# Attention before a routed expert layer: keys and queries turned on VectorE, 32x32 score tiles, one early expert phase

## The chip, the core and the metric

The kernel runs on one core of a Trainium2 chip. It uses TensorE (PE: matmuls and transposes), VectorE (DVE), ScalarE (ACT), GpSimd (POOL), SyncE (SP) and 16 DMA engines. The metric is the time on the device from the start to the end of one execution, in microseconds (us); lower is better. Profile and times come from different executions.

## What is computed

Eight batches of eight heads with 576 tokens of 64 dimensions, 32 rows p for each head. First p attends to k and v, which gives 32 packed rows a head; then every q attends to the packed rows. The result, 4608 rows of 512, goes through a layer of eight experts, of which each row takes the best one.

```python
def sm_attn(qq, kk, vv):
    s = scale * np.matmul(qq, kk.transpose(0, 1, 3, 2))
    s = s - np.max(s, axis=-1, keepdims=True)
    a = np.exp(s)
    a = a / (np.sum(a, axis=-1, keepdims=True) + 1e-09)
    return np.matmul(a, vv)
p_packed = sm_attn(p, k, v)
out = sm_attn(q, p_packed, p_packed)
...
logits = x @ w_gate + modality_bias[modality_id]
e_idx = np.argmax(logits, axis=1)
...
    h = np.maximum(x[mask] @ w1[e], 0.0)
    out[mask] = gate_w[mask, None] * (h @ w2[e])
```

Everything is fp32. With the data of the runs the rows go to three of the eight experts.

## The kernel before

**Attention.** The eight batches are four pairs, the heads two groups of four: eight units of work (pair i, group g), each 2 batches x 4 heads x 576 tokens. `load_tok` brings k and q of a unit as 128 partitions x 4 tokens (512 tokens of a batch, L199, runs of 1024 B) and the 64 left-over tokens of both batches apart (L195, runs of 256 B); `load_v` does the same for v (L220, L222). `relayout` copies each batch's tokens so that heads come behind tokens, k on ACT (L207), q on DVE (L209). `trans` turns them on PE, three 128x128 transposes at a time (L229), and ACT copies the turned block out of PSUM (L233). `scores1` multiplies p's rows with the turned keys (L242, tiles of 64 columns), takes the maximum (L247), the negated maximum (L250) and the exponential with its sum (ACT, L254). `a1trans` turns the weights on PE (L266), ACT copies them (L269), `pack` multiplies them with v (L279, tiles of 32 columns) and divides by the sum (L284, into `bd`, where every head stands in its own half). `packT` turns the packed rows (L293), `gate` gives the heads' share of the logits (L304). `scores2` multiplies packed rows and turned queries (L315). DVE turns the scores by 32x32 blocks (L321), takes the maximum over the 32 packed rows (L324), subtracts (L326), ACT takes the exponential (L328), DVE sums (L331), adds 1e-9 and inverts (L333, L335), multiplies (L337) and turns back (L340). `xpart` multiplies with `bd` (L354): 128 columns of x and 8 of logits. ACT copies x out (L362), DVE the logits (L366), SP writes x to the scratch tensor `x_scr` in DRAM (L374, L379).

**Routing.** For each pair `routing` adds up the logits (L423), takes the best expert, ranks the rows of an expert by a scan and a matmul, and scatters each row's number and weight into the expert's list `lst` by nine indirect DMAs on POOL (L467).

**Experts.** Work is cut into *slots*: two tiles of 128 rows of one expert; with this data there are 20, three of them of one tile only. `table_phase` works out on DVE which slot is whose. `fetch` reads the slot's list (`mt`, L657) and gathers its rows of x (L659, two indirect DMAs) on POOL. `st_x` turns the rows on PE (L672) and splits them in a high and a low part (ACT L674, DVE L675); `st_1` does x @ w1 as three products of parts (L685), with relu and split (L689, L690); `st_2` does the second product (L719), the weight (L723) and the indirect write of the rows (L724). For three one-tile slots there is another form (L703). Expert weights come by SP (2 MB each) and are split by ACT (L652) and DVE or POOL (L653) into `w1h`, `w1l`, `w2h`, `w2l`.

**Order.** PE, DVE, ACT and SP take their instructions in program order. For the attention the order is the string `ORDER` (L404 to L408), walked once a unit; a `>` before a step's name means the unit one later. The experts run in three phases (`NA`, `SA`): phase a has two slots and needs the rows of the first two pairs only, phase b goes on to slot 6 with the rows of three pairs, phase c takes the rest. So slots 0 and 1 stand in PE's program ahead of the last attention units, whose steps follow between their matmuls (`run_all`).

## Time and profile before

| | |
|---|---|
| three runs | 643.27, 644.70 and 644.98 us, median 644.7 |
| the profiled execution, first to last instruction | 658.5 us |
| PE busy in it | 598.8 us |
| DVE, ACT, POOL busy | 261.5, 238.6, 156.2 us |
| DMA bytes | 87.11 MB |
| mean granted TensorE clock | 0.961 |

The profiled execution is longer than the runs without a profile; sums against the trace are made in its own time. Busy time is that of any instruction on the engine. A row of a timeline reads: start, length, engine, line, operation, output <- input, shape, count, and in brackets the idle time before it and what ended that. A row of groups reads: line, engine, operation, output <- input, forms, count, then busy time, mean ns of one, and the idle time just before them with its releasers. PE's tile sizes stand as rows*columns.

### The profile page before, as it was taken

The numbers are of one execution on the slowest core, as the hardware profiler recorded it, in microseconds if no ns is written. First come the engines' busy times: TensorE is split into PE (matmuls) and PEld (weight loads), VectorE is DVE, ScalarE is ACT, GpSimd is POOL, SyncE is SP. The second block draws the span as 40 slices with busy tenths as digits, with TensorE's granted clock in tenths as the row PEclk, the third lists the DMA queues.
The fourth block names the chain that finished last, engine by engine and source line by source line (L and its number), as shares of the span: only waits on it lengthen the run. The fifth ranks groups of instructions, "written<-read, shape, count | busy, mean of one in ns | idle before, by whom it ended". The sixth has DMA issues, their size and how long they took to land. (4 is left out here: it accounts for less than half of the span.)

```text
span 658.5 us, 12203 instructions
## 1 busy us (share of the span) xinstructions
PE 598.8 (91%) x4564; PEld 505.9 (77%) x4564; DVE 261.5 (40%) x670; ACT 238.6 (36%) x457; POOL 156.2 (24%) x204
## 2 busy tenths in 40 slices
PE   3899969868689989999999999999999999999983
PEld 3565646535478968889888988998899899889982
DVE  1488958769955422112612016311120121112181
ACT  4677847756612202121612127221121221222271
POOL 3001050256161171211221322221122112122121
PEclk9999988968779998999999999999999999999998
DMA  9989999934843811111590212720110111112011
GB/s 239 277 200 274 314 303 300 292 92 146 317 148 105 295 30 63 49 49 33 198 397 30 66 50 66 290 66 34 50 49 34 50 50 53 45 50 51 35 50 53
DMA packets 74856, 87.11 MB, mean 132 GB/s; under 512 B 26448, under 2 KB 60240, under 8 KB 74768
## 3 DMA queue, kind: packets, MB, share of 16 engines
q1 hardware_dynamic: 64656, 63.79, 32.6%
q0 software_dynamic: 8528, 21.93, 10.6%
q8 instruction: 47, 0.77, 0.5%
q10 hardware_dynamic: 1584, 0.28, 0.2%
q14 instruction: 41, 0.34, 0.2%
HBM read 66.74 MB, written 19.24 MB: 131 GB/s over the span
## 5 line engine op out<-in xcount | busy, mean ns | idle before, releaser
L685 PE MATMUL ps_h<-x_hl,w1h 128*128 128x256 f32 x1088 | 202.1, 287 | 5.7 <-issue 4.9
L685 PEld LDWEIGHTS ps_h<-x_hl,w1h 128*128 128x128 f32 x1088 | 174.4, 195 | 8.5 <-issue 5.9
L685 PE MATMUL ps_h<-x_hl,w1l 128*128 128x256 f32 x544 | 155.8, 286 | 0.9 <-issue 0.8
L690 DVE SCALAR_TENSOR_TENSOR hl<-ps_h,hh 128x512 fp32r<-128x512 f32 x68 | 46.9, 690 | 263.8 <-ACT hh L689 261.4
L719 PE MATMUL ps_o<-w2h,hh 128*128 128x512 f32 x296 | 118.0, 399 | 2.8 <-ACT ot L723 1.6
L719 PE MATMUL ps_o<-w2h,hl 128*128 128x512 f32 x296 | 116.8, 395 | 0.0
L719 PE MATMUL ps_o<-w2l,hh 128*128 128x512 f32 x296 | 115.8, 391 | 0.3 <-DVEq L844 0.3
L685 PEld LDWEIGHTS ps_h<-x_hl,w1l 128*128 128x128 f32 x544 | 106.1, 195 | 1.5 <-issue 1.4
L689 ACT ACTIVATE hh<-ps_h 128x512 fp32r<-128x512 f32 x68 | 40.6, 597 | 179.0 <-PE ps_h L685 148.0
L724 POOL DMA_INDIRECT out_dram<-ot,mt x37 | 40.5, 1096 | 189.0 <-ACT ot L723 120.7
L723 ACT ACTIVATE ot<-ps_o,mt 128x512 f32<-128x512 f32 x37 | 25.4, 687 | 141.3 <-PE ps_o L719 115.1
L659 POOL DMA_INDIRECT xt<-x_scr,mt x46 | 45.0, 979 | 104.0 <-PE ps_t L672 45.2
L719 PEld LDWEIGHTS ps_o<-w2h,hh 128*128 128x128 f32 x296 | 55.7, 188 | 14.2 <-ACT ot L723 2.5
L719 PEld LDWEIGHTS ps_o<-w2h,hl 128*128 128x128 f32 x296 | 55.6, 188 | 11.6
L719 PEld LDWEIGHTS ps_o<-w2l,hh 128*128 128x128 f32 x296 | 55.7, 188 | 10.9 <-DVEq L844 0.6
L233 ACT COPY kT<-ps 128x384 f32<-128x384 f32 x96 | 44.0, 489 | 37.7 <-PE ps L229 20.4
L467 POOL DMA_INDIRECT lst<-meta,dsi x36 | 35.3, 980 | 83.2 <-DVE starts L522 31.4
L675 DVE TENSOR_TENSOR x_hl<-ps_t,x_hl 128x512 fp32r<-128x512 f32 x42 | 27.5, 683 | 19.7 <-ACTq L844 14.8
L229 PE MATMUL ps<-ident,rek 128*128 128x128 f32 x144 | 25.7, 306 | 10.3 <-POOL meta L114 7.0
L354 PE MATMUL ps<-bd,a2T 64*128 64x136 f32 (+1 forms) x320 | 28.7, 313 | 5.0 <-DVE lt L366 4.7
L657 POOL DMA_DIRECT2D mt<-lst x23 | 17.3, 752 | 61.9 <-DMA out_dram<-ot,mt 48.2
L229 PEld LDWEIGHTS ps<-ident,rek 128*128 128x128 f32 x144 | 17.9, 154 | 17.0 <-POOL meta L114 7.0
(189 smaller groups left out, 706.4 us busy)
## 6 DMA issues: line engine op xcount, KB each, us to landing
raw<-in_moe_w_dram SPq DMA_DIRECT2D x24, 1024.0 KB
raw<-in_k_dram SPq DMA_DIRECT2D x16, 512.0 KB
raw<-in_q_dram SPq DMA_DIRECT2D x16, 512.0 KB
ld_v<-in_v_dram SPq DMA_DIRECT2D x16, 512.0 KB
x_scr<-xs SPq DMA_DIRECT2D x16, 512.0 KB
rek<-in_k_dram SPq DMA_DIRECT2D x16, 64.0 KB
req<-in_q_dram SPq DMA_DIRECT2D x16, 64.0 KB
ld_v<-in_v_dram SPq DMA_DIRECT2D x16, 64.0 KB
```

Source lines behind the costliest of these rows:

```text
L229: nc.tensor.transpose(out=t[:, c * P:c * P + P], in_=D_[nm + "r"][:, c0 + c, 2 * pr:2 * pr + 2, :], identity=ident)
L233: nc.scalar.copy(out=T_[:, pr, c0 * P:c0 * P + 3 * P], in_=t[:, :3 * P])
L354: nc.tensor.matmul(xp[rows, pr, z * XW:z * XW + XW], a2T[rs, t0:t0 + n], D_["bd", u][rs, :], start=True, stop=True)
L467: ins = ins_of(nc.gpsimd.indirect_dma_start(out=lst, out_offset=bass.IndirectOffsetOnAxis(ap=dsi[:, c:c + 1], axis=0), in_=meta[:, i * NC ...
L659: ins.append(nc.gpsimd.indirect_dma_start(out=xt[:, t], out_offset=None, in_=x_scr[0:NA[ph] * 2 * S] if ph < 2 else x_scr, in_offset=bass. ...
L675: iv = tt(out=M["xl"][:, :, ts], in0=ps, in1=M["xh"][:, :, ts].bitcast(F32), op=ALU.subtract)
L685: nc.tensor.matmul(ps[:, f], M[a][:, j, (f0 + f) * P:(f0 + f) * P + P], M[b][:, j], start=(n == 0), stop=(n == 3 * KD - 1))
L689: ia = nc.scalar.activation(out=M["hh"][:, fs], in_=ps, func=AF.Relu)
L690: iv = nc.vector.scalar_tensor_tensor(out=M["hl"][:, fs], in0=ps, scalar=0.0, in1=M["hh"][:, fs].bitcast(F32), op0=ALU.max, op1=ALU.subtract)
L719: nc.tensor.matmul(op, M[a][:, j, t * P:t * P + P], M[b][:, j, :], start=(n == 0), stop=(n == 3 * KF - 1))
L723: nc.scalar.activation(out=ot, in_=op, func=AF.Copy, scale=mt.bitcast(F32)[:, t, 2:3])
L724: nc.gpsimd.indirect_dma_start(out=out, out_offset=bass.IndirectOffsetOnAxis(ap=mt[:, t, 1:2], axis=0), in_=ot, in_offset=None, bounds_che ...
```

## The change

**Loads.** All three tensors come as 64 partitions x 9 tokens for each batch, two batches one above the other (new `load`, L212, runs of 2304 B, two DMAs a tensor). The left-over tokens and the copies of `relayout` are gone. x is kept in two scratch tensors, one for each group of heads, and written by one DMA a unit (new L366, 9360 B a partition).

**Turning.** Instead of PE's transposes and ACT's copies, DVE turns k and q by 32x32 blocks (new `turn`, L220, 128x1152, four for each unit). A head dimension of 64 then lies in two blocks of 32 partitions.

**Scores.** New `scores` (L230) makes both score products from 32x32 tiles: 32 matmuls of 288 columns, 16 positions, two accumulated (64 instructions in the trace, as fp32 matmuls are counted twice). The packed product (L285) and the x product (L354) use 64x64 tiles.

**Second softmax.** The scores come out with tokens in the free dimension in the order that the x product wants. The maximum is a reduce with transposition (L331, four a unit, 128x9 from 128x288), spread by a transpose of a broadcast input (L335); one subtraction (L339) and one exponential (L344) follow. x is stored undivided, with two sums of weights for each pair of heads, got as two more columns of `bd` (`XW` = 130). `routing` divides the logits (L393 to L402) and `st_x` the rows of x (L659 to L662: add, reciprocal, multiply) before it turns them.

**Gathers.** `fetch` has four gathers a slot (L645, a tile from each of the two scratch tensors) where there were two.

**Phases.** One early phase b (three pairs, six slots) replaces a and b. All of attention and the routing of all four pairs stand ahead of the first expert matmul in PE's program.

The core of the diff:

```diff
-    NA = (NP // 2, NP - 1)
-    SA = [max(0, -((E * (P2 - 1) - m * 2 * S) // P2)) for m in NA]
+    NA = NP - 1
+    SA = -((E * (P2 - 1) - NA * 2 * S) // P2)
...
+        def load(src, nm):
...
+            for u in range(2):
+                nc.sync.dma_start(t[64 * u:64 * u + 64].rearrange("p h c d -> p h (c d)"),
+                                  src[2 * i + u, hs].rearrange("h (p c) d -> p h (c d)", c=NC))
...
+        def turn(nm, z):
...
+            nc.vector.transpose(out=D_[nm + "T"][:, 2 * z:2 * z + 2].rearrange("p h c b q -> p (h c b q)"),
+                                in_=D_[nm][:, 2 * z:2 * z + 2].rearrange("p h c d -> p (h c d)"))
...
+        def scores(l, r, nm):
+            t = [ps.tile([P, 2, 512], F32, name="ps") for u in range(2)]
+            for db in range(2):
+                for h in range(HG):
+                    for u, hf in QD:
+                        qd = slice(32 * (2 * u + hf), 32 * (2 * u + hf) + 32)
+                        nc.tensor.matmul(t[u][32 * h:32 * h + 32, hf, :HS].rearrange("p (c q) -> p c q", c=NC),
+                                         l[qd, db, 32 * h:32 * h + 32], r[qd, h, :, db, :],
+                                         start=(db == 0), stop=(db == 1), skip_group_check=True)
...
+            for hf in range(2):
+                nc.vector.tensor_reduce(m2[:, hf], s2[:, hf, :HS].rearrange("p (c q) -> p c q", c=NC),
+                                        axis=AX.X, op=ALU.max, apply_transpose=True)
...
+            nc.vector.transpose(out=mB.rearrange("p f c q -> p (f c) q"),
+                                in_=m2.rearrange("p f c -> p (f c)")[:, :, None].broadcast_to([P, 2 * NC, 32]))
...
+            nc.vector.tensor_tensor(out=a2.rearrange("p c f q -> p f c q"),
+                                    in0=s2[:, :, :HS].rearrange("p f (c q) -> p f c q", c=NC), in1=mB,
+                                    op=ALU.subtract)
...
-        for t in range(2):
-            ins.append(nc.gpsimd.indirect_dma_start(
-                out=xt[:, t], out_offset=None, in_=x_scr[0:NA[ph] * 2 * S] if ph < 2 else x_scr,
+        for t in (1, 0):
+            for g in range(2):
+                ins.append(nc.gpsimd.indirect_dma_start(
+                    out=xt[:, t, g], out_offset=None, in_=x_scr[g] if ph else x_scr[g][0:NA * 2 * S],
...
+            nc.vector.tensor_scalar_add(rs[:, :, :, 0], xr[:, :, P:XW], 1e-9)
+            nc.vector.reciprocal(rs, rs)
+            xn = M["xn", t]
+            tt(out=xn.rearrange("p (a h d) -> p a h d", a=4, h=2), in0=xr[:, :, 0:P].rearrange("p a (h d) -> p a h d", h=2),
+               in1=rs.broadcast_to([P, 4, 2, D]), op=ALU.mult)
...
+            if i == NA - 1:
                 E0.append(val(E0[1], 0, 0, (ET.SP,), 0, E - 1))
                 load_w(W, 0, E0[2])
...
+                T.append((yield from table_phase("b", E0[0], NA, None, SA)))
...
+                for n in range(2):
+                    pre(n)
+                    yield
+                for z in range(4):
+                    split_w(W, 0, nc.gpsimd, (z,))
+                    yield
```

**DVE in a unit.** Before, from the second scores of one unit to its last turned block (`st` is the score block, `m` its maximum, `dn` the sum, `mx` and `nb` belong to the next unit's first softmax):

```order
L321 STREAM_TRANSPOSE st<-ps_1009 128x288 x2
L326 TENSOR_TENSOR st<-st,m_1023 128x576
L247 TENSOR_REDUCE mx<-ps_1036 128x1
L250 TENSOR_SCALAR nb<-mx 128x1
L331 TENSOR_REDUCE dn<-st 128x18
L247 TENSOR_REDUCE mx<-ps_1045 128x1
L333 TENSOR_SCALAR dn<-dn 128x18
L250 TENSOR_SCALAR nb<-mx 128x1
L324 TENSOR_REDUCE m_1079<-st 128x18
L335 RECIPROCAL dn<-dn 128x18
L326 TENSOR_TENSOR st<-st,m_1079 128x576
L337 TENSOR_TENSOR st<-st,dn 128x576
```

Now, from the spread packed rows (`pc`, what packT turns) to the unit's last subtraction (`a2T`, L339); the two L242 are the next unit's:

```order
L183 TENSOR_TENSOR pc<-bd_119 128x2x64 x2
L242 TENSOR_REDUCE nb<-ps 128x1
L220 STREAM_TRANSPOSE qT<-raw 128x1152
L242 TENSOR_REDUCE nb<-ps 128x1
L220 STREAM_TRANSPOSE kT<-raw 128x1152
L331 TENSOR_REDUCE m_609<-ps 128x9 x2
L331 TENSOR_REDUCE m_612<-ps 128x9 x2
L335 STREAM_TRANSPOSE mB<-m_609 128x576
L335 STREAM_TRANSPOSE mB<-m_612 128x576
L253 TENSOR_SCALAR r_556<-r_556 128x2
L254 RECIPROCAL r_556<-r_556 128x2
L339 TENSOR_TENSOR a2T<-ps,mB 128x2x9x32 x2
```

The exchange of sums and divisions for turns of k and q is seen here; the maximum of the next unit's first softmax stands between the turns.

**PE in a unit.** Before, from one unit's x products to the next one's first scores:

```order
L354 MATMUL ps_694<-bd,a2T 128x136 x4
L229 MATMUL ps_699<-ident,rek 128x128 x3
L229 MATMUL ps_703<-ident,rek 128x128 x3
L315 MATMUL ps_718<-kT,ppT 64x288 x4
L229 MATMUL ps_723<-ident,rek 128x128 x3
L229 MATMUL ps_733<-ident,rek 128x128 x3
L315 MATMUL ps_739<-kT,ppT 64x288 x4
L229 MATMUL ps_744<-ident,req 128x128 x3
L229 MATMUL ps_756<-ident,rek 128x128 x3
L242 MATMUL ps_761<-kT,pT 64x288 x4
```

Now a whole unit:

```order
L268 MATMUL ps<-ident,a_787 128x128 x8
L354 MATMUL ps<-bd_119,a2T 64x146 x24
L274 MATMUL ps<-ident,a_787 128x128
L354 MATMUL ps<-bd_119,a2T 64x146 x12
L285 MATMUL ps<-ld_v,a1T 64x128 x36
L230 MATMUL ps<-kT,pT 32x288 x32
L301 MATMUL ps<-ident,pc 128x128 x2
L314 MATMUL ps<-wg_124,ppT 32x16 x16
L230 MATMUL ps<-qT,ppT 32x288 x32
```

The transposes of k and q between the scores are gone; the first scores of a unit stand right behind the packed product of the one before.

**POOL before the first slots.** Before, the scatters of two pairs, the low parts of the first weights, and the lists and gathers of slots 0 and 1 (nine scatters of the third pair come behind them):

```order
L467 DMA lst<-meta,dsi 38912x4 x18
L653 TENSOR_TENSOR w1l<-raw_114,w1h 128x4x256 x4
L628 TENSOR_LOAD tab_a
L657 ISA
L657 DMA mt_2321<-lst 128x2x4
...
L659 DMA xt_2325<-x_scr,mt_2321 128x512 x2
L659 DMA xt_2326<-x_scr,mt_2322 128x512 x2
```

Now:

```order
L449 DMA lst<-meta,dsi 38912x4 x27
L638 TENSOR_TENSOR w1l<-raw_115,w1h 128x4x256 x2
L613 TENSOR_LOAD tab_b
L642 ISA
L642 DMA mt_100<-lst 128x2x4
...
L645 DMA xt_104<-x_scr_63,mt_100 128x260
L645 DMA xt_104<-x_scr_64,mt_100 128x260
...
L645 DMA xt_105<-x_scr_63,mt_101 128x260
L645 DMA xt_105<-x_scr_64,mt_101 128x260
L449 DMA lst<-meta,dsi 38912x4 x3
```

Ahead of the first list there are now the scatters of three pairs, and eight gathers in place of four ahead of the first expert matmul; in DVE's program the routing of pairs 1 to 3 and both tables stand behind the last unit's L339 (pair 1's from its second half on).

More of the change, by code (lines that the diff above doesn't have):

```diff
@@ L59, in packed_attn_moe_kernel @@
     sm = ctx.enter_context(tc.tile_pool(name="sm", bufs=4))
-    x_scr = dram.tile([N, DM], F32, name="x_scr")
+    XW = P + 2
+    XL = XW + 2 * E
+    GW = 2 * XW
+    x_scr = [dram.tile([N, GW], F32, name=f"x_scr{g}") for g in range(2)]
     lst = dram.tile([E * R, 4], I32, name="lst")
@@ L170, in prep_p @@
-    def prep_p(ps1, n4):
-        t = ps1.tile([P, 512], F32, name="ps1")
+    bds = [cw.tile([P, 2, XL], F32, name=f"bd{n}") for n in range(2)]
+    for t in bds:
+        for u in range(2):
+            nc.gpsimd.tensor_copy(out=t[:, u, P:XW], in_=mask[:, :, 0])
+    wg4 = cw.tile([P, 2, HG, 2, 2, E], F32, name="wg4")
+    nc.gpsimd.memset(wg4, 0.0)
+    wgt = cw.tile([P, 4 * HG, E], F32, name="wgt")
+    nc.gpsimd.memset(wgt, 0.0)
+    for u in range(2):
+        nc.scalar.dma_start(wgt[64 * u:64 * u + 32], w_gate.rearrange("(n p) e -> p n e", p=32))
@@ new lines, in packed_attn_moe_kernel, with more, step @@
+        todo = [rest()]
+        def more():
+            while todo:
+                try:
+                    next(todo[0])
+                    return
+                except StopIteration:
+                    todo.pop(0)
+        def step(m, nm):
+            next(us[m][nm])
+            if m == 0 and nm == "dk":
+                load_p(nc.scalar, 0, 2)
+                load_p(nc.scalar, 2, NP)
+            if m == 1 and nm == "dk":
+                for _ in prep_p(A["ps"], 2, nc.gpsimd):
+                    pass
+            if m == 0 and nm == "k0":
+                for _ in prep_p(A["ps"], 0, nc.vector):
+                    pass
+            if nm == "w0" and m % 2 and m // 2 < NA:
+                todo.append(route(m // 2))
```

562 lines of the change are left out of this document (243 added, 319 removed), and 4 rows, old and new, of the table ORDER.

## The prediction

> **What bounds the kernel now.** The page first: engines, then the slices.
>
> ```profile
> span 658.5 us, 12203 instructions
> PE 598.8 (91%) x4564; PEld 505.9 (77%) x4564; DVE 261.5 (40%) x670; ACT 238.6 (36%) x457; POOL 156.2 (24%) x204
> PE   3899969868689989999999999999999999999983
> DMA  9989999934843811111590212720110111112011
> ```
>
> PE is busy almost throughout, but for two reasons. The DMA row is full for some ten slices (attention) and nearly empty later (experts). The windows by stage separate them: one attention unit (from one pack's end to the next), the first expert slots after the attention, and eight later slots.
>
> ```profile
> 59.87:78.47 18.60, 17.13 (x213) 11.08 (x211) 15.70 (x43) 13.66 (x32) 0.00 (x0) 1.00 1.10 315
> 240.00:262.00 22.00, 18.00 (x116) 17.11 (x115) 2.21 (x4) 3.14 (x6) 8.12 (x9) 0.84 0.16 49
> 431.36:617.40 186.04, 186.04 (x1211) 169.68 (x1210) 31.68 (x48) 37.86 (x64) 37.80 (x40) 1.00 0.15 47
> ```
>
> After the length the columns are PE, PEld, DVE, ACT, POOL, granted clock, DMA share, GB/s. The eight slots leave PE no gap: 186.04/8 = **23.3 us a slot**, and the change leaves these matmuls alone (the same 20 slots in the same order). In the attention the DMA engines are over 100% busy with PE close behind. So the change can act on when the experts start and on their first slots, not on their rate.
>
> ```profile
> 181.02 1.01 PE L685 MATMUL ps_h<-x_hl,w1h 128*128 128x256 f32 x3
> 240.57 0.40 PE L685 MATMUL ps_h<-x_hl,w1h 128*128 128x256 f32 x2
> 244.07 0.40 PE L685 MATMUL ps_h<-x_hl,w1h 128*128 128x256 f32 x2 [1.13 <-issue]
> 246.18 0.60 PE L685 MATMUL ps_h<-x_hl,w1h 128*128 128x256 f32 x2 [1.59 <-issue]
> ```
>
> The first expert matmul is at 181.0. Slots 0 and 1 last until slot 2 starts at 240.57: 59.6 us where two slots alone take 46.5, because the last attention units run between their matmuls. From 240.57 to the span's end are **417.9 us**. At its head slot 2 stalls and runs at a lower clock (0.84 in the window), 6 to 7 us in all.
>
> **The new attention unit.** The old ones end their packs (L284) here:
>
> ```profile
> 22.78 0.61 DVE L284 SCALAR_TENSOR_TENSOR bd<-ps,r,mask 128x128 f32<-128x128 f32 x2 [2.02 <-PE ps L279]
> 42.32 0.59 DVE L284 SCALAR_TENSOR_TENSOR bd<-ps,r,mask 128x128 f32<-128x128 f32 x2
> 59.87 0.57 DVE L284 SCALAR_TENSOR_TENSOR bd<-ps,r,mask 128x128 f32<-128x128 f32 x2
> 78.47 0.58 DVE L284 SCALAR_TENSOR_TENSOR bd<-ps,r,mask 128x128 f32<-128x128 f32 x2
> 102.08 0.57 DVE L284 SCALAR_TENSOR_TENSOR bd<-ps,r,mask 128x128 f32<-128x128 f32 x2
> ```
>
> So 17.5 to 19.5 us a unit, and 23.6 where a pair's routing falls in. Transfers first:
>
> ```profile
> q1 hardware_dynamic: 32326, 25.74, 102.1%
> q1 hardware_dynamic: 1286, 3.28, 87.2%
> ```
>
> The first row is the attention from 50 to 140 us (packets, MB, share): 25.74/(90 x 1.021) = 280 GB/s in runs of 1024 and 256 B, 16.8 us for a unit's 4.72 MB. The second is an expert's weights, 335 to 345 us, in 4096 B packets: 376 GB/s. The new loads have runs of 2304 B, the x writes 9360 B; between the two rows I take 354 GB/s, **13.4 us** for 4.74 MB. [...]
>
> The work that goes, and the rows for what comes:
>
> ```profile
> L229 PE MATMUL ps<-ident,rek 128*128 128x128 f32 x144 | 25.7, 306 | 10.3 <-POOL meta L114 7.0 <-DMA rek<-in_k_dram 2.2 <-ACT rek L207 0.5
> L229 PE MATMUL ps<-ident,req 128*128 128x128 f32 x144 | 25.5, 299 | 1.7 <-issue 1.6
> L233 ACT COPY kT<-ps 128x384 f32<-128x384 f32 x96 | 44.0, 489 | 37.7 <-PE ps L229 20.4 <-remote 6.7 <-issue 6.1
> L207 ACT COPY rek<-raw 128x1024 f32<-128x1024 f32 x16 | 16.4, 1086 | 3.8 <-DMA raw<-in_k_dram 3.8
> L321 DVE STREAM_TRANSPOSE st<-ps 128x288 f32<-128x288 f32 x32 | 13.5, 459 | 13.7 <-remote 11.8 <-PE ps L315 1.8
> L340 DVE STREAM_TRANSPOSE a2T<-st 128x576 f32<-128x576 f32 x16 | 12.4, 777 | 0.4 <-DVEq L826 0.3
> L247 DVE TENSOR_REDUCE mx<-ps 128x1 f32<-128x576 f32 x16 | 12.1, 755 | 15.7 <-remote 8.9 <-PE ps L304 3.3 <-PE ps L242 3.0
> L326 DVE TENSOR_TENSOR st<-st,m 128x576 f32<-128x576 f32 x16 | 12.0, 750 | 0.1
> L324 DVE TENSOR_REDUCE m<-st 128x18 f32<-128x576 f32 x16 | 11.9, 741 | 0.0
> L284 DVE SCALAR_TENSOR_TENSOR bd<-ps,r,mask 128x128 f32<-128x128 f32 x16 | 4.7, 330 | 2.0 <-PE ps L279 2.0
> 45.67 1.19 PE L315 MATMUL ps<-kT,ppT 128*64 128x288 f32 x8
> 55.77 1.62 PE L279 MATMUL ps<-ld_v,a1T 128*32 128x64 f32 x80
> ```
>
> Gone are 51 us of PE's transposes (L229) and 60 of ACT's copies (L233, L207): over eight units 6.4 and 7.6 us each. ACT is then far from bounding. DVE becomes the chain of a unit. From the end of a pack to the last subtraction (new L339) it does, in its order: two products and two spreads (0.33 each by L284: 1.3), maximum (0.76), one turn of q, maximum (0.76), one turn of k, four reduces with transposition, two broadcast transposes (0.78 each by L340: 1.6), the reciprocal (0.3) and two subtractions (0.75 by L326: 1.5). A turn of 1152 columns isn't in the trace: 288 columns take 459 ns and 576 take 777, so 1.10 ns a column, 1.41 us each, 2.8 for two (bounds: 1.2 and 2.8 for both, from one column a ns and from two passes). Nor is a reduce that transposes: half of L324 is 0.37, that and a transpose (L321) 0.83; I take 0.41, 1.6 for the four, since the transpose alone costs no more than a pass. Sum **10.6 us**.
>
> The next pack waits for that subtraction: both want a PSUM buffer, and of the four the ninth allocation of a unit falls on what L339 reads. Then PE does the last transpose of the weights, a third of the x products and the pack of 72 instructions. L279 needs 1.62/80 = 20 ns an instruction with four tiles at once; by that spacing, stretched to 128 columns, 72 x 0.028 = 2.0, and 1.4 for the rest: 3.4. The other two turns (2.8) lie under these 3.4. So **T = 14.0 us a unit**, DVE busy for 13.4 of it, transfers 13.4.
>
> The scores now are 64 instructions in 32x32 tiles. L279 shows four column tiles at once, L315 two columns of 64 (0.149 us each, 0.30 for one tile's stream). Sixteen at once: 64 x 0.30/16 = 1.2 us; four: 4.8. I take 1.3 (64 x 20 ns), hidden behind the spreads, as the row shows column tiles running apart. [...]
>
> **Until the last unit.** The first pack's end stays at 22.8: the same first loads, two turns in place of copies and transposes. Seven units to 120.8, 10.6 to the subtraction, and 4 of routing that lie on DVE (the period with routing was 5 longer): sub(7) at **135.4**.
>
> **The tail.** Nothing of the experts is on PE before now. Its pieces are POOL's:
>
> ```profile
> 125.24 0.96 POOL L467 DMA_INDIRECT lst<-meta,dsi  x1 [31.39 <-DVE starts L522]
> 126.50 0.96 POOL L467 DMA_INDIRECT lst<-meta,dsi  x1 [0.30 <-issue]
> 136.78 4.66 POOL L653 TENSOR_TENSOR w1l<-raw,w1h 128x1024 fp32r<-128x1024 f32 x2
> 154.91 1.56 POOL L657 DMA_DIRECT2D mt<-lst  x2
> 158.92 1.03 POOL L659 DMA_INDIRECT xt<-x_scr,mt  x1 [2.44 <-DMA mt<-lst]
> 163.15 0.94 POOL L659 DMA_INDIRECT xt<-x_scr,mt  x1 [0.30 <-issue]
> L423 DVE TENSOR_REDUCE lg<-lt 128x72 f32<-128x288 f32 x4 | 2.6, 652 | 0.1
> L430 DVE TENSOR_TENSOR eq<-eq,desc 128x72 f32<-128x72 f32 x4 | 0.9, 234 | 0.1
> L675 DVE TENSOR_TENSOR x_hl<-ps_t,x_hl 128x512 fp32r<-128x512 f32 x42 | 27.5, 683 | 19.7 <-ACTq L844 14.8
> ```
>
> The rest of routing(1), some 20 dependent instructions (0.65, then 0.23 to 0.45) and a step on PE: 6.6. Eighteen scatters at 1.26: 22.8. Two w1l 4.7, two mt 1.6, again 4.7 and 1.6; table b on DVE (some 90 instructions of 0.2) is done by then. Four gathers of slot 0, 5.2, and four of slot 1, 5.2: DVE divides slot 1's rows before the second half of slot 0, so both count. Landing 2.4 (the wait in the 158.92 row), two divisions and the second low part 2.5 (0.68 each and two small ones). Sum **57.3**: first full expert matmul at 192.7, 11.7 after before's. On the way PE idles.
>
> Nothing then lies between slots 0 and 1: 46.5 in place of 59.6. Slot 2's stall partly goes; a cold clock at the experts' start and the doubled gathers come. Of the 6 to 7 us I give back 2.5 (bounds 0 and 5). Span: 192.7 + 46.5 + 417.9 - 2.5 = **654.6 us**, against 658.5. The runs had a median of 644.7, 0.979 of the profiled span: **641 us**, 0.6% less. The end is the same: the last slot, with its output, is in the 417.9.
>
> **Rivals.**
> - *Slower: the reduces with transposition (L331).* At the upper bound of 0.83 they add 1.7 us to the chain, eight times: 13.5 us, 668, **654**. They decide from 0.2 us each on, as everything after waits. For it: both operations are full passes in the rows; against: the transpose L321 is itself a pass of the same length as a reduce.
> - *Slower: 32x32 tiles in fours.* The scores take 4.8; DVE waits 3.5 after the spreads and 1.5 before the reduces, 5 us a unit, 35 in all: **675**. It counts from 1.3 us on. For it: no row has small tiles in both directions; against: each direction alone overlaps.
> - *The change doesn't do what it says:* the loads stay at 280 GB/s, a unit at 16.8 to 17: 21 us more, 676, **661**. [...] Against it stand the weights' 376 GB/s.
> - *Faster:* PE and DVE follow at the starts' spacing, T = 13.3 (5 us less), and slot 2's whole stall goes (4): 645.6, **632**. For it: in the rows of one engine starts lie some 0.07 closer than the durations; against: before's units were 0.7 to 2.7 over their largest need of 16.8.
>
> **How the numbers follow.** Forecast 0.40 (637 to 646), faster rival 0.20, reduces 0.20, loads 0.10, tiles 0.07, others 0.03. A measurement of this kernel can tell 0.3% from no change, 2 us. Faster takes 0.28 of the forecast and the faster rival: 0.48. Same takes 0.10 and a part of the rivals' near ends: 0.15. Slower the rest: 0.37. The range runs from 629 (a little beyond the faster rival) to 661, and leaves the tiles out above and the rest below.
>
> **What would show it.** A pack every 14.0 us with DVE over 90% busy and q1 above 340 GB/s; scores in 1.3 us; reduces (L331) at 0.41; 18 scatters in one row after the last subtraction, then w1l, mt and eight gathers; the first expert matmul near 193, slot 2 about 46 to 48 us later, and from there the same 23.3 a slot. Wrong it is if the units run over 15.5 us, or if scatters of pair 1 already run under the last units (the tail then shrinks by up to 11), or if slot 2 still stalls.

## The result and the profile after

| | before | after |
|---|---|---|
| median of the runs, us | 643.99 (4 runs) | 739.99 (4 runs, 732.47 to 746.33) |
| profiled execution, span, us | 658.5 | 744.6 |

The change makes the kernel slower: ratio 1.145, 95% interval 1.138 to 1.152. The ratio leaves out the slowest of after's runs, 746.33 us, and that one is the profiled execution. A few us of its 744.6 are therefore its own: two kernels below with the same attention have their last subtraction at 175.6 and 175.8 us, after has it at 179.6. What is said below of causes rests on the experiments too. The forecast was 641 us, with a range from 629 to 661.

The forecast was 654.6 us of span, so 90 us are to be found. First the page of after: busy time, then the slices for PE, the granted clock and the DMA engines.

```profile
span 744.6 us, 13666 instructions
PE 573.0 (77%) x5428; PEld 491.0 (66%) x5428; DVE 295.0 (40%) x649; ACT 188.4 (25%) x339; POOL 201.5 (27%) x234
PE   2676566686101999999987599799999999999871
PEclk9879876988555799999998799799999999999997
DMA  9999969952636401111390111451111111112111
```

PE had 91% before and has 77% now. It is half idle in the first ten slices, where the DMA row is full, and idle for two slices behind them (the tail). Small holes stand in the experts. Each of the three is placed by a few rows of the timeline: the subtractions of the attention units (DVE, start and length), then POOL and PE.

```profile
40.37 1.40 DVE L339 TENSOR_TENSOR a2T<-ps,mB 128x576 f32<-128x576 f32 x2
58.00 1.40 DVE L339 TENSOR_TENSOR a2T<-ps,mB 128x576 f32<-128x576 f32 x2
...
179.63 1.42 DVE L339 TENSOR_TENSOR a2T<-ps,mB 128x576 f32<-128x576 f32 x2
209.27 0.96 POOL L449 DMA_INDIRECT lst<-meta,dsi  x1 [0.30 <-issue]
210.26 4.64 POOL L638 TENSOR_TENSOR w1l<-raw,w1h 128x1024 fp32r<-128x1024 f32 x2
217.99 0.80 POOL L642 DMA_DIRECT2D mt<-lst  x1 [3.10 <-DVE ends L505]
238.02 1.09 PE L666 MATMUL ps_t<-ident,xn 128*128 128x128 f32 x4 [38.22 <-DVE xn L662]
244.31 0.58 PE L679 MATMUL ps_h<-x_hl,w1h 128*128 128x256 f32 x1 [1.22 <-DVE x_hl L669]
```

Slot 2 begins at 293.78, by its first product with w1, as in the prediction. So these are the windows of slot 0, of slot 1 and of all behind them, and below them before's window behind slot 1 (PE is the first busy time, the granted clock the third number from the end):

```profile
244.31:270.20 25.89, 25.55 (x151) 23.28 (x152) 6.75 (x16) 4.04 (x7) 11.72 (x13) 0.90 0.25 69
270.20:293.81 23.61, 23.22 (x154) 20.97 (x153) 5.76 (x12) 4.73 (x8) 6.64 (x7) 1.00 0.15 46
293.81:744.60 450.79, 403.94 (x2569) 364.13 (x2567) 129.92 (x242) 109.14 (x178) 121.76 (x124) 0.95 0.22 71
240.57:658.50 417.93, 397.76 (x2569) 361.40 (x2567) 101.00 (x144) 108.17 (x178) 90.71 (x93) 0.98 0.23 77
```

The last subtraction ends at 181.0 where 135.4 was forecast: **45.6 us in the attention**. Of these, 8.4 lie ahead of the first subtraction's end (41.8, by the prediction 22.8 + 10.6 = 33.4), the rest in the units ((179.63 - 40.37)/7 = 19.9 us a unit, not 14.0, or 14.6 with the routing). From there to the first full expert matmul at 244.3 are 63.3 us, forecast 57.3: **6 in the tail**. Slots 0 and 1 take 49.5 (forecast 46.5): **3**. From 293.8 to the end are 450.8, forecast 417.9 - 2.5: **35.4 in the other slots**. The sum is 90. Against before's 417.9, PE is idle 27 us longer there, and its same 2569 matmuls take 6 us more, at a granted clock of 0.95 instead of 0.98.

What the loads do in the attention, from 40 to 140 us: the row of their queue (packets, MB, share of 16 engines), then the window.

```profile
q1 hardware_dynamic: 11458, 21.61, 94.7%
```

```profile
40.00:140.00 100.00, 64.03 (x1416) 42.41 (x1417) 57.82 (x99) 30.03 (x67) 2.50 (x5) 0.80 0.96 218
```

The DMA engines are as full as in before, but move **218 GB/s** where before's moved 280. PE is busy for 64 of 100 us and DVE for 58: neither bounds. PE's holes there have no releaser; two of them, the second the longest:

```profile
61.22 1.03 PE L354 MATMUL ps<-bd,a2T 64*64 64x146 f32 x19 [3.53 <-issue]
116.02 2.45 PE L230 MATMUL ps<-kT,pT 32*32 32x288 f32 x47 [6.92 <-issue]
```

The groups by line of the new operations (count, then busy time, mean ns, idle time ahead of them):

```profile
L220 DVE STREAM_TRANSPOSE qT<-raw 128x1152 f32<-128x1152 f32 x16 | 21.8, 1361 | 8.0 <-DMA raw<-in_q_dram 8.0
L331 DVE TRANSPOSE_TENSOR_REDUCE m<-ps 128x9 f32<-128x288 f32 x32 | 12.5, 450 | 13.4 <-PE ps L230 13.4
L230 PE MATMUL ps<-kT,pT 32*32 32x288 f32 x512 | 17.9, 475 | 11.6 <-issue 11.6
L354 PE MATMUL ps<-bd,a2T 64*64 64x146 f32 x576 | 28.9, 338 | 11.4 <-issue 7.8 <-DVE a2T L339 2.2 <-ACT a1T L270 1.3
```

The turn took 1.36 us (I said 1.41), the reduce with transposition 0.45 (0.41). DVE's terms were right. The "issue" ahead of L230, L354, L285 and L314 sums to some 37 us. In the trace, DVE waits for PE far more than for a load: from 40 to 160 us, 26.8 us for scores and 10.3 for packs, and 4.2 for q. So the rows alone don't say whether the transfers or PE's holes set the period; the experiments must.

In the experts PE waits 29.8 us from slot 2 on in holes of over 0.7 us. One of them, as rows of PE and of DVE:

```profile
425.18 1.12 PE L666 MATMUL ps_t<-ident,xn 128*128 128x128 f32 x4 [7.13 <-DVE x_hl L669]
424.22 0.28 DVE L659 TENSOR_SCALAR rx<-xt 128x8 f32<-128x8 f32 x2 [11.42 <-DMA xt<-x_scr,mt]
424.43 0.69 DVE L669 TENSOR_TENSOR x_hl<-ps_t,x_hl 128x512 fp32r<-128x512 f32 x1
```

DVE stands 11.4 us at L659, the first operation of the division, until a gather has landed. The next in its order, 0.2 us later, is a low part (L669) for which PE has been waiting. The gathered rows belong to a later slot, the low part to a nearer one. DVE took them in its program order, so this late gather of a later slot stopped PE for 7.1 us.

### The profile page after: what moved, and what is told of

Its sections match the earlier page's. It is cut to its first block, busy times and chain, and to the rows that moved or that the text cites. A ratio compares the mean times of both kernels' runs of the same rounds, so it can differ in the third digit from the quotient of the medians.

```text
span 744.6 us, 13666 instructions
## 1 busy us (share of the span) xinstructions
PE 573.0 (77%) x5428; PEld 491.0 (66%) x5428; DVE 295.0 (40%) x649; ACT 188.4 (25%) x339; POOL 201.5 (27%) x234
## 3 DMA queue, kind: packets, MB, share of 16 engines
q1 hardware_dynamic: 24960, 58.95, 29.4%
## 5 line engine op out<-in xcount | busy, mean ns | idle before, releaser
L679 PE MATMUL ps_h<-x_hl,w1h 128*128 128x256 f32 x1088 | 199.2, 285 | 2.6 <-DVE x_hl L669 1.2
L713 PE MATMUL ps_o<-w2h,hh 128*128 128x512 f32 x296 | 120.0, 406 | 3.7 <-ACT ot L717 2.3
L713 PE MATMUL ps_o<-w2l,hh 128*128 128x512 f32 x296 | 117.5, 397 | 0.9 <-DVEq L844 0.9
L645 POOL DMA_INDIRECT xt<-x_scr,mt x92 | 89.4, 971 | 84.3 <-DMA mt<-lst 22.7
L666 PE MATMUL ps_t<-ident,xn 128*128 128x128 f32 x168 | 30.1, 311 | 65.0 <-DVE xn L662 45.0
L666 PEld LDWEIGHTS ps_t<-ident,xn 128*128 128x128 f32 x168 | 22.9, 159 | 72.0 <-issue 38.5
L662 DVE TENSOR_TENSOR xn<-xt,rx 128x512 f32<-128x512 f32 x42 | 27.7, 688 | 27.4 <-PE ps_t L666 27.2
L354 PE MATMUL ps<-bd,a2T 64*64 64x146 f32 x576 | 28.9, 338 | 11.4 <-issue 7.8
L354 PEld LDWEIGHTS ps<-bd,a2T 64*64 64x64 f32 x576 | 22.2, 159 | 17.1 <-issue 13.0
L659 DVE TENSOR_SCALAR rx<-xt 128x8 f32<-128x8 f32 x42 | 6.0, 170 | 68.2 <-DMA xt<-x_scr,mt 68.2
## 6 DMA issues: line engine op xcount, KB each, us to landing
x_scr<-xs SPq DMA_DIRECT2D x8, 1170.0 KB, 10.6
raw<-in_k_dram SPq DMA_DIRECT2D x16, 576.0 KB, 11.4
ld_v<-in_v_dram SPq DMA_DIRECT2D x16, 576.0 KB, 14.5
```

The source lines that it names most:

```text
L354: nc.tensor.matmul(xp[64 * u:64 * u + 64, pr, c * XL:c * XL + XL], a2T[rs, 3 * z + c, u], bd[rs, u, :], start=True, stop=True, skip_group_ ...
L645: ins.append(nc.gpsimd.indirect_dma_start(out=xt[:, t, g], out_offset=None, in_=x_scr[g] if ph else x_scr[g][0:NA * 2 * S], in_offset=bass ...
L659: nc.vector.tensor_scalar_add(rs[:, :, :, 0], xr[:, :, P:XW], 1e-9)
L662: tt(out=xn.rearrange("p (a h d) -> p a h d", a=4, h=2), in0=xr[:, :, 0:P].rearrange("p a (h d) -> p a h d", h=2), in1=rs.broadcast_to([P, ...
L666: nc.tensor.transpose(out=ps[:, j], in_=xn[:, j * P:j * P + P], identity=ident)
L679: nc.tensor.matmul(ps[:, f], M[a][:, j, (f0 + f) * P:(f0 + f) * P + P], M[b][:, j], start=(n == 0), stop=(n == 3 * KD - 1))
```

## The experiments

Ratios stand to runs of the kernel before on the same chip. A difference to after, or between kernels of different chips, is taken from the ratios, at 643 us; after has 1.145.

**Loads alone.** The first question was why 218 and not 354 GB/s. Nothing but loads of k, in several forms, read by one DVE copy each.

```diff
+    def load_d(t, src, i, g):   # 64 partitions, runs of 2048 B
+            nc.sync.dma_start(t.rearrange("p (h x) -> p h x", h=HG)[64 * u:64 * u + 64, :, 0:512],
+    def load_f(t, src, i, g):   # 128 partitions, runs of 2048 B
+            nc.sync.dma_start(t.rearrange("p (u k x) -> p u k x", u=2, k=2)[:, u, :, 0:512],
```

> Nothing is computed here: seven groups of 8 loads of k, each group waiting for the one before, each in another form; the output is zeros plus one number. In the changed kernel the loads ran at 218 GB/s (64 partitions, runs of 2304 B), before at 288 (128 partitions, 1024 B, with some 256 B). Theory H (half the partitions): a load that fills only 64 partitions at a time is slow. Then group 1 (64 x 2304 B, as in the change) about 220 GB/s, group 2 (both halves at once, from two queues) over 300, group 3 (128 x 2304 B) over 300, group 4 (64 x 2048 B) about 220, group 5 (128 x 1024 B) 280 to 320, groups 6 and 7 (128 x 2048 and 128 x 4608 B) over 340. Theory L (the run length of 2304 B): groups 1, 2 and 3 about 220, group 4 over 330 as groups 6 and 7.

The windows of the third group (128 partitions, 2304 B) and the fourth (64 partitions, 2048 B); the last two numbers are DMA share and GB/s:

```profile
82.00:103.00 21.00, 1.08 (x7) 0.00 (x0) 1.00 1.06 392
105.00:142.00 37.00, 1.17 (x8) 0.00 (x0) 1.00 1.07 230
```

Groups 5 to 7 (128 partitions, 1024, 2048 and 4608 B) ran at 387 to 412. So the run's length plays little part here between 1024 and 4608 B; the partitions do. Both rows show full engines, at 392 and at 230: the share doesn't tell the rate. Group 2's second queue (ACT, always the upper half) began at once, beside group 1; the 16 tiles of both took 80 us, 235 GB/s together. By the bytes of the queues, SP's was still in group 1 up to 56 us and filled lower halves behind that:

```profile
45.00:58.00 13.00, 0.31 (x2) 0.00 (x0) 1.00 1.05 219
58.00:64.00 6.00, 0.31 (x2) 0.00 (x0) 1.00 1.06 363
```

From 58 to 64 us SP's queue moved 1.09 MB into lower and ACT's 1.09 MB into upper halves: 363 GB/s. So two transfers into opposite halves, both in flight, aren't held to the half rate.

**The loads away from the kernel.** k, q and v are loaded once and used eight times, so every unit works on the first unit's data and the experts get other rows.

```diff
+            if nm in ONCE:
+                D_[nm] = ONCE[nm]
+                yield
+                return
```

> The changed kernel with k, q and v loaded for the first unit only; all units compute on those, so the rows differ. If the transfers set the unit (20.3 us now), the period falls to that of the chain of DVE and PE: 14.0 by the prediction, 16 to 17 with the score tiles as they ran (64 in 2.5 us); the last subtraction then comes at 140 to 152 instead of 181, the time is 30 to 40 us shorter. If not the transfers but PE's own gaps without a releaser set it, the period stays at 19 or more and the time moves by less than 12 us. If those gaps come from instructions that arrive late behind the loads, they fall from some 37 us in the attention to under 10.

671.1 us (1.042), 66 less than after. The pack's rows on DVE (L296 in this kernel) and the last subtraction (L345):

```profile
67.60 0.61 DVE L296 SCALAR_TENSOR_TENSOR bd<-ps,r,mask 128x128 f32<-128x128 f32 x2 [0.57 <-ACT a2T L350]
80.90 0.61 DVE L296 SCALAR_TENSOR_TENSOR bd<-ps,r,mask 128x128 f32<-128x128 f32 x2 [0.58 <-ACT a2T L350]
...
136.06 1.42 DVE L345 TENSOR_TENSOR a2T<-ps,mB 128x576 f32<-128x576 f32 x2
```

Without loads a unit takes 12.9 to 13.3 us (15.1 and 19.5 where a pair's routing falls in), the first steps begin later, and the last subtraction starts at 136.1. The chain of 14.0 was right, a little long. PE's "issue" ahead of scores and x products is gone as well. Of the 66 us only 44 lie ahead of the last subtraction; 29 lie behind the first full matmul (471.1 instead of 500.3), where the experts get other rows, so that nothing follows from them.

**The division away.** The rows of x go undivided to PE (left out: L659 to L662).

```diff
-            nc.vector.tensor_scalar_add(rs[:, :, :, 0], xr[:, :, P:XW], 1e-9)
-            nc.vector.reciprocal(rs, rs)
...
-                nc.tensor.transpose(out=ps[:, j], in_=xn[:, j * P:j * P + P], identity=ident)
+                nc.tensor.transpose(out=ps[:, j], in_=xr[:, j, 0:P], identity=ident)
```

> The changed kernel without the division of the gathered rows (42 x add, reciprocal, multiply, 1.8 us for a tile and its neighbour); PE turns the gathered rows directly, so the rows are not divided. Theory D: in the expert slots the rows come late at changes of expert, and the division stands in the chain behind them: the gaps of PE there (30 us) shrink by 1.5 to 2 us at each of seven places, 10 to 15 us less in all, 725 to 730. Rival G: the four gathers and the wait for the list set it: less than 5 us.

701.99 us (1.092), 34 less than after. From the first full matmul (236.1) to the end (698.0) are 461.9 us, which is what the prediction's terms give (46.5 + 415.4; here 50.1 for slots 0 and 1, and 411.8); after takes 500.3. The loss in the other slots hangs on the division, and with its holes the lower clock goes too: 0.98 over the stretch, 0.95 in after.

**Only its place in DVE's order.** The division is kept behind the low part of the slot ahead of it.

```diff
+            if "xl_last" in M:
+                tc.add_manual_dep(ir, M["xl_last"].name, SYNC, reason="behind the rows before")
...
+        M["xl_last"] = ins_of(iv)
```

> The changed kernel with one more dependency: the first division step of a slot's rows stands behind the last low part (x_hl) of the slot before, so that it is no longer ahead of it in DVE's order. The work is the same. Theory O (order on DVE: the division of the slot after next waits for its gathers ahead of the low part that PE needs next): PE's gaps in the slots fall from 30 us to under 8, the time by 25 to 38 us, as without the division (702). Rival W (the work and the length of the division's chain): as the changed kernel, within 8 us.

717.81 us (1.117), 18 less than after. The holes in the slots fall from 29.8 to 14.5 us, the stretch from the first full matmul from 500.3 to 477.8. Of the loss in the experts order is 18 us by the ratios and 22 in the traces; 16 stay, by both, until the division goes. What is left of the holes ends for the most part on the division itself, 10.3 of 14.5 us; one of them:

```profile
447.95 1.26 PE L668 MATMUL ps_t<-ident,xn 128*128 128x128 f32 x8 [3.60 <-DVE xn L664]
```

**Half of the gathers**, on top of this (half of x is left out, constant data in its place).

```diff
-            for g in range(2):
+            for g in range(1):
```

> e5 (717.8) with two gathers a slot instead of four: the second group of heads isn't gathered (its columns keep a constant), so half of x is wrong and half the bytes move. Theory G: what is left of PE's gaps in the slots after the order is mended (14 us: at the change of expert and the last slots) comes from gathers that end 2.5 us later; they fall to 7 or less, and with the tail's 5 us of gathers the time falls by 10 to 14: 704 to 708. Rival: the division's chain alone; then only the tail gains, 4 to 6 us.

707.2 us (1.102), 10 less. The first expert matmul comes 7 us earlier, at 231.0; the holes stay at 15.5 us. The doubled gathers cost at the tail only.

**Routing earlier**, on top of the order: two steps of routing at each place in the string instead of one.

```diff
                             more()
+                            more()
```

> e5 (717.8), and the waiting routing steps taken two at a time, so that 18 scatters stand ahead of the last unit's end and 9 behind it. Theory P (POOL's row is the tail): first expert matmul 8 to 12 us earlier, 704 to 711. Rival (DVE's tables are the tail, or the routing steps delay the units): within 4 us of e5.

721.43 us (1.121), no gain. It didn't do what was meant: still nine scatters, not 18, stand ahead of the last subtraction, though they begin at 146.5 instead of 161.2. The last subtraction starts at 179.35 instead of 175.76. Behind it ACT waits 9.0 us for the first expert's weights (until 197.32), DVE 8.5 us for an ACT step of the routing that stands behind those weights (until 201.40), and the last nine scatters for DVE.

**The same bytes in other ways.** Half of each load on ACT's queue:

```diff
-                nc.sync.dma_start(t[64 * u:64 * u + 64]
+                (nc.sync, nc.scalar)[u].dma_start(t[64 * u:64 * u + 64]
```

> The changed kernel with the second batch's half of every load issued on ACT's queue instead of SP's, so that both halves of the partitions are filled at once. Theory H: the loads run at 290 GB/s or more, the last subtraction comes 15 to 35 us earlier and the time falls by that. Theory L: the same rate, within 4 us of the changed kernel. What speaks against a gain in both: ACT issues 24 loads between its copies (some 0.6 us each).

764.34 us (1.187), 27 more than after. The loads of both queues together move 191 GB/s between 40 and 120 us, and ACT issues its half late: the first subtraction starts at 52.05 instead of 40.37. On POOL's queue instead, with the edits of order and routing:

> e10, and the second batch's half of each load issued on POOL's queue, which is idle there, so that both halves of the partitions fill at once. Theory H: 280 to 320 GB/s (300 in the load study with two queues), period 16 to 17, the last subtraction at 145 to 160, 20 to 35 us less than e10: 672 to 690. Rival: as on ACT's queue (e3), no gain, within 6 us of e10.

705.2 us (1.100), 16 less than without it, and the last subtraction 5.8 us earlier; both theories missed. 223 GB/s between 40 and 120 us, where after and the kernel with the order have 213: in this kernel the second queue hardly raised the rate. Why it doesn't, where loads alone had 363 with opposite halves, isn't shown, nor where the other 10 us come from; 9 of them lie behind the first full matmul.

One head in each transfer, over all 128 partitions:

```diff
-                nc.sync.dma_start(t[64 * u:64 * u + 64].rearrange("p h c d -> p h (c d)"),
-                                  src[2 * i + u, hs].rearrange("h (p c) d -> p h (c d)", c=NC))
+            for h in range(HG):
+                nc.sync.dma_start(t[:, h].rearrange("p c d -> p (c d)"),
+                                  src[2 * i:2 * i + 2, HG * g + h].rearrange("u (p c) d -> u p (c d)", c=NC))
```

> The changed kernel with every load cut by heads instead of by batches: four DMAs a tensor, each into all 128 partitions (same tiles, same runs of 2304 B). Theory H (a load into 64 partitions runs at half the rate: 222 against 390 GB/s in the load study): the loads of a unit take 9 to 11 us instead of 16, the period falls from 20 to 13 to 14 us as without loads, the last subtraction comes at 135 to 142 instead of 180, PE's gaps without a releaser in the attention go: 40 to 48 us less, 692 to 700. If the loads' rate is set by something else in this kernel (the x writes, the instructions' own fetches), less than 15 us.

1152.91 us (1.792). It tested something else than meant. In the row of its queue, 40 to 120 us:

```profile
q1 hardware_dynamic: 1786, 4.06, 13.1%
```

4.06 MB in 80 us is 51 GB/s at 13.1% of the time of 16 engines, as much as two engines have. Here the source's outermost dimension is the two batches; whether that is the reason isn't shown. The next two kernels have the same loads and say nothing beyond that (1128.69 and 1130.99 us):

> Both edits, e4 and e5. If the two costs are separate they add: 740 - 45 - 35 = 655 to 665, and the run stands where the prediction's sum stood (654.6 in the profiled span) plus what the tail is longer (some 5): a span of 655 to 662. If they share a cause, less than 60 us of gain together.

> e6, and the waiting routing steps are taken two at a time, so that the scatters of pairs 0 and 1 (18) stand ahead of the last unit's end and only 9 of pair 2 behind it. Theory P (the tail is POOL's row of scatters, lists and gathers): the first expert matmul comes 8 to 13 us earlier than in e6 against the last subtraction, and the time falls by that, to 643 to 652. Rival: DVE's tables set the tail, or the routing steps lengthen the units by what the tail gains: within 4 us of e6.

**All 128 partitions in one piece.** Two heads of a batch lie one behind the other in DRAM, so one transfer can fill 128 partitions with 128 rows at one distance. It exchanges the places of heads and batches; the work is the same, the data aren't.

```diff
-                nc.sync.dma_start(t[64 * u:64 * u + 64].rearrange("p h c d -> p h (c d)"),
-                                  src[2 * i + u, hs].rearrange("h (p c) d -> p h (c d)", c=NC))
+                nc.sync.dma_start(t[:, 2 * u:2 * u + 2].rearrange("p k c d -> p k (c d)"),
+                                  src[2 * i + u, hs].rearrange("h s d -> (h s) d").rearrange(
+                                      "(k p c) d -> p k (c d)", k=2, c=NC))
```

> The changed kernel with loads that fill all 128 partitions in runs of 2304 B, two DMAs a tensor as now: partitions 64 to 127 hold the second head of a pair instead of the second batch, so heads and batches are exchanged in what is computed; the work is the same. (e4 meant to show this, but its loads ran at 51 GB/s, each on two of the 16 DMA engines.) Theory H: loads at 330 to 390 GB/s, period 13 to 15 us instead of 20, PE's gaps without a releaser in the attention under 12 us instead of some 37, the last subtraction at 136 to 145 instead of 180, some 40 us less in all (the experts' rows differ). Rival: the loads' rate or those gaps have another cause; the last subtraction stays later than 165.

711.78 us (1.107), 25 less than after. Its last subtraction (L340):

```profile
143.48 1.42 DVE L340 TENSOR_TENSOR a2T<-ps,mB 128x576 f32<-128x576 f32 x2
```

Two of its windows:

```profile
40.00:80.00 40.00, 32.04 (x866) 21.08 (x869) 35.30 (x61) 17.75 (x42) 0.00 (x0) 0.96 0.85 278
80.00:120.00 40.00, 28.87 (x709) 19.78 (x705) 30.02 (x54) 17.58 (x39) 2.50 (x5) 0.84 0.86 319
```

The last subtraction comes 36 us earlier (32 against the 175.6 of the kernels with the same loads as after), the DMA engines are no longer full, DVE is busy for 35 and 30 of 40 us, and the "issue" falls from 37 to 8 us. The first full expert matmul stands at 207.1, 37 us ahead of after's. Together with the order:

> e8_full_width_mixed (heads and batches exchanged, so other data in the experts) together with the order of e5_order: both causes found so far taken away. If they are independent: the full expert matmul starts near 207 as in e8_full_width_mixed, the slots lose the 22 us of e5_order, so 711.8 - 22 = 690. If the order's gain there was already smaller, because the data give other slots: 695 to 705. If both hid a third cause: below 680.

Here before itself had 658.2 us, so only ratios compare: 1.0994 (1.0922 to 1.1066), against 1.1068 (1.1008 to 1.1127) without the order. The intervals overlap; the two gains don't add up. With these data the order saves some 8.5 us of holes in the slots (22.0 to 13.5). But in this profile the last subtraction starts at 153.65, 10.2 us later, with the same attention:

```profile
146.20 0.61 DVE L291 SCALAR_TENSOR_TENSOR bd<-ps,r,mask 128x128 f32<-128x128 f32 x2 [10.60 <-issue]
```

From 136.4 to 143.2 us PE gets the pack's matmuls in small groups, 1.4 us apart, each with an "issue" of 0.2 to 1.0 us, while the DMA engines are at 15% of their time. There are 10 us more of "issue" from 229 to 239 us, and a wait for the tables of 11.0 us in place of 6.8. So it is these holes that hide the gain; what causes them isn't shown, and full DMA engines can't be it here.

**Which partitions.** Is it the number of partitions, the place, or the size of a transfer? Again loads alone, and beside them after's kernel with order, and lower and upper half by turns:

```diff
+            for h in range(HG):
+                for u in range(2):
+                    nc.sync.dma_start(t[64 * u:64 * u + 64, h].rearrange("p c d -> p (c d)"),
+                                      src[2 * i + u, HG * g + h].rearrange("(p c) d -> p (c d)", c=NC))
```

> Only loads of k (nothing else is computed): five groups of eight transfers into 128x2304 tiles, one queue, read by VectorE in turn. Group 1 is the change's form: 64 partitions x 4 runs of 2304 B, first the lower half of the partitions, then the upper; it was 222 GB/s, 5.3 us for 1.18 MB, before. Group 2 the same bytes in eight transfers of one head, lower and upper half by turns. Group 3 four transfers into 32 partitions each. Group 4 partitions 32 to 95, 0.59 MB a tile. Group 5 four transfers of one head pair over all 128 partitions. Theory of the partitions (a transfer reaches only the part of the memory's write side that its partitions belong to, so the rate goes with the partitions in flight): group 3 near 110 to 150 GB/s, group 4 near 220 if any 64 partitions count alike, group 5 near 390, group 2 up to 390 if neighbours in a queue overlap and 222 if they don't. Rival (a transfer with fewer descriptors for each engine has a fixed cost in between): group 2 and 5, with smaller transfers, are slower than group 1, and group 4 as group 1.

Windows inside the five groups: halves as in the change, halves by turns, 32 partitions, partitions 32 to 95, all 128.

```profile
5.00:45.00 40.00, 1.07 (x7) 0.00 (x0) 1.00 1.05 222
47.00:75.00 28.00, 0.77 (x5) 0.00 (x0) 1.00 0.96 245
82.00:128.00 46.00, 1.12 (x8) 0.00 (x0) 1.00 1.04 229
128.00:139.50 11.50, 1.25 (x9) 0.00 (x0) 1.00 1.06 392
141.00:162.00 21.00, 1.25 (x8) 0.00 (x0) 1.00 1.05 392
```

Both theories missed: 32 partitions are no slower than 64, and 64 at another place are as fast as 128. The fourth group differed in place and form, so the place was changed alone:

> Only loads of k, nothing else is computed: five groups of eight tiles, the same transfers (runs of 2304 B, two heads each, two to a tile), to different partitions: 0 to 63, 32 to 95, 0 to 31, 48 to 79, 64 to 127; 0.59 MB a tile where there are 64 partitions, 0.295 where there are 32. In m2_loads_halves partitions 32 to 95 had 391 GB/s and 32 or 64 partitions within one half 222. Theory of the halves (a transfer is limited to about 222 GB/s within partitions 0 to 63 or 64 to 127, however many of them it uses, and to about 390 if it spans both sides of 64): a tile takes 2.65 us, 1.5, 1.33, 0.75 to 0.85 (or 1.33 if the 32 partitions of 48 to 79 reach only half of each side), 2.65. Rival (the transfers of two heads made the fourth group of m2_loads_halves fast, not its place): all of 64 partitions 1.5.

Partitions 0 to 63, 32 to 95, 0 to 31, 48 to 79, 64 to 127:

```profile
5.00:25.00 20.00, 0.88 (x6) 0.00 (x0) 1.00 1.05 205
28.00:37.00 9.00, 0.86 (x6) 0.00 (x0) 1.00 1.06 392
38.00:49.00 11.00, 0.99 (x7) 0.00 (x0) 1.00 1.06 204
50.00:61.00 11.00, 1.01 (x7) 0.00 (x0) 1.00 1.05 202
65.00:83.00 18.00, 0.90 (x6) 0.00 (x0) 1.00 1.05 206
```

The place decides. 0 to 63 and 64 to 127 have half the rate (205 and 206 GB/s), and 0 to 31 no less (204); 32 to 95 has all of it (392). 48 to 79 crosses the middle and still has half (202). So neither the number of partitions nor crossing the middle alone sets the rate; what does, the runs don't show.

> e5_order with each load cut into eight transfers of one head, lower and upper half of the partitions by turns in the same queue. Theory of the partitions with overlap of neighbours: loads go from 220 to above 300 GB/s, the unit's period from about 20 to 15 to 16, the last subtraction from 176 to 145 to 150, and the time from 717.8 to about 690. If neighbours in a queue don't overlap: period 20 as before, time 715 to 720. Rival of a fixed cost for each transfer: period longer than 20.5, time above 722.

704.18 us (1.0995), 11 less than with the order alone, and with POOL's queue (1.100) the lowest among the kernels that leave nothing out and exchange nothing. Its window from 40 to 120 us, and behind it that of the kernel with the order alone:

```profile
40.00:120.00 80.00, 57.18 (x1396) 40.78 (x1396) 52.29 (x89) 30.39 (x67) 2.51 (x5) 0.87 0.75 218
```

```profile
40.00:120.00 80.00, 54.16 (x1179) 35.77 (x1179) 45.41 (x75) 24.99 (x58) 2.52 (x5) 0.78 0.96 213
```

The DMA share falls from 0.96 to 0.75 at no fewer bytes. PE's "issue" is gone in the groups between 30 and 150 us (30 us with the order alone), and the last subtraction starts at 163.94 instead of 175.76. That is less than the 145 to 150 expected. DVE now waits for loads; the first row is DVE's turns of k, the second the issuing of one tensor on SP:

```profile
L221 DVE STREAM_TRANSPOSE kT<-raw 128x1152 f32<-128x1152 f32 x16 | 21.9, 1370 | 20.7 <-DMA raw<-in_k_dram 20.7
58.47 5.95 SPq L213 DMA_DIRECT2D raw<-in_k_dram  x8
```

A transfer of one head is 0.147 MB. SP took 5.95 us to issue these eight, 0.74 us each, which is 198 GB/s; in the loads alone eight landed every 4.65 to 4.84 us, 0.58 to 0.60 us each. That SP's issuing sets the 245 and the 218 by turns was the author's estimate and isn't shown, and neither run tells whether neighbours in a queue overlap. But this run settles the question from the result: with PE's "issue" gone the unit still takes 17.6 us ((163.94 - 40.81)/7), now waiting for loads. PE's holes lay largely in the transfers' shade.

No version ran faster than before; 704 stands against 642.

## Why the prediction was wrong, step by step

- **The loads, the first step that failed.** "The new loads have runs of 2304 B ...; between the two rows I take 354 GB/s". The rate was read as one of run length. Both rows came from transfers to 128 partitions (but for the left-over tokens of before), the new ones go to one half. They ran at 218 GB/s, 4.74 MB in 21.7 us instead of 13.4, so the transfers and not DVE's chain became a unit's period. The rival ("the loads stay at 280 GB/s") had the right place, and at 21 us too low a price, since 280 was taken as the floor. Shown by the load-only runs and by the kernel with full-width loads, whose last subtraction comes 32 to 36 us earlier.
- **The first unit, a term too small.** "The first pack's end stays at 22.8": it was 30.1, and the first subtraction ended at 41.8 instead of 33.4. With full-width loads it still ends at 39.3, so some 6 of the 45.6 us in the attention are not the loads' rate.
- **The chain, right.** T = 14.0 was 12.9 to 13.3 once the loads were gone. Turn, reduces, spread and subtraction took what was said. The rival of the slow reduces falls (0.45 us, not 0.83), and the one of tiles in fours too.
- **Scores and pack, sizes off.** 1.3 us were said for 64 small matmuls; after has 2.2 (k) and 3.1 (q) on the mean, the kernel without loads mostly 1.6 and 2.5. The pack took 3.0 on the mean where 2.0 was said, mostly 2.15 without loads. Both lie beside DVE's work.
- **The tail, 63.3 for 57.3.** Scatters, low parts and gathers follow as said. The last scatter is over 29.2 us after the subtraction, 29.4 in the sum. "Table b ... is done by then" failed: the first `mt` waits for the table (3.10 <-DVE ends). In the rows, DVE loses 5.2 us on the way to it at an operation on one element, which ends together with POOL's first low parts:

```profile
209.56 5.35 DVE L586 SCALAR_TENSOR_TENSOR pref<-pref,tab_f 1x1 f32<-1x1 f32 x1
```

  A second one, on 128x8 elements (L606), stands beside the next low parts (219.08, 5.33 us); others of these sizes take 0.14 to 0.32. Beyond that, 2.8 us were missing from the last gather to the first full matmul (7.7 for 4.9).
- **Slots 0 and 1, 3 us too short**: 49.5 for 46.5. Slot 1 took 23.6 at a full clock, slot 0 25.9 at a granted clock of 0.90, behind 0.50 from 200 to 244 us, where PE was busy for 3.0. The prediction names "a cold clock at the experts' start", and gave 2.5 us back in spite of it.
- **The rest of the slots, the second step that failed: a term put at nothing.** The sum takes before's 417.9 for all behind slot 1. The division of slots 2 to 19 stands in it at nothing, without a reason, and what stands behind its wait in DVE's order isn't asked. It cost 34 to 38 us: order 18 to 22, the division's own chain between a late gather and PE's turn another 16. "The doubled gathers", which the prediction names, weren't the reason: half of them changed no hole. In before, PE took the gathered rows directly, and its transposes of x (L672) had only 2.2 us of idle time ahead of them in the whole run.
- **PE's "issue"**, not foreseen. 37 us in after, 31 to 32 in the other kernels with the same loads on SP, 26 with half on POOL's queue, 8 with full width, none without loads or by turns. But half-rate loads don't always bring it (1.6 us with half on ACT's queue), and it came with quiet DMA engines too (full width with the order, 136 to 143 us). What PE lacks there the trace doesn't name; that its instructions come late past the loads' queues isn't shown.
- **The factor 0.979.** It was before's alone: after's profiled span stood at 1.006 of its median, and the experiments' profiled executions within 1% of theirs. With after's own factor the forecast would have been 10 us higher, above before's median. The terms taken from before's trace, the 417.9 above all, may thus be 2% long.
- **Still open.** No run has both causes wholly taken away with the same data. From two runs an estimate: 207.1 to the first full matmul (full-width loads) and 461.9 behind it (no division) give 669 us, more than before has. That is 14 more than the forecast's span: some 6 in the first unit, 4 in the others, 5 in the tail. So the sign would have been missed without the two causes as well, and the 641 were in part luck of the factor; the tail, in which PE waits 37 to 38 us in one piece, is the first place to look, but it wasn't taken away in a run.

## What to carry to other kernels

Before a load's layout is changed, look at which partitions each single transfer writes, not only at its run length: here transfers to the lower or upper 64 partitions ran at 205 to 230 GB/s where 128 partitions had 392, both at full DMA share. When an operation that waits for a DMA is put on an engine, look up what stands behind it in the program's order, and put it behind the work of the slots ahead (DVE stood 11.4 us at L659 with the low part behind it; the edge that turned the two gave 18 us). An engine's busy share showed neither: DVE had 40% before and after. Before many small transfers are put in place of a few, count what the issuing engine needs for each (SP took 5.95 us for eight).

## What the runs showed of the hardware

- A load to partitions 0 to 63, 64 to 127, 0 to 31 or 48 to 79 ran at 202 to 230 GB/s, to 32 to 95 or all 128 at 392, in one queue; run lengths from 1024 to 4608 B changed little (387 to 412 on 128 partitions).
- Lower and upper half by turns in one queue, 0.147 MB each: 245 GB/s, eight landing every 4.65 to 4.84 us. Lower half from SP's queue and upper from ACT's, loads alone: 363 GB/s over 6 us.
- Half of each load from a second queue, in the kernel: 223 GB/s with POOL's and 191 with ACT's, against 213 to 218 with SP's alone. Loads alone had 363 GB/s with both halves in flight, against 219 just before.
- A load whose source has an outermost dimension of two went at 51 GB/s, with 13.1% of the time of 16 engines.
- A matmul in a 32x32 tile with 288 columns took 25 to 40 ns of PE's time each where 64 follow one another (1.6 to 2.5 us, without loads).
- On DVE an operation on one element took 5.35 us and one on 128x8 elements 5.33 us, beside POOL's low parts of 4.64 and 4.65 us, ending with them; others of these sizes take 0.14 to 0.32.
